# Retention and a routed MLP on one core: the order of loads, weights and gathers around the first batches

## The chip, the core and the metric

The kernel runs on one core of a Trainium2 chip. Its engines are TensorE (PE in the profile, with its weight loads as PEld), VectorE (DVE), ScalarE (ACT), GpSimd (POOL) and SyncE (SP), and a core has 16 DMA engines. The metric is the device time of one execution in microseconds, lower is better; times are medians of several executions.

## The reference

Two blocks follow each other. The first is retention in its parallel form: 8 batches, 8 heads, 576 positions, head size 64. The second is a mixture of depths: of each batch's 576 tokens the 128 with the highest gate score go through an MLP (512 to 1024 to 512), and all others pass unchanged. All is float32.

```python
scores = scale * np.matmul(q, k.transpose(0, 1, 3, 2))
Dmat = np.where(rel >= 0, gamma[:, None, None] ** rel[None, :, :], 0.0)
attn_out = np.matmul(scores * Dmat[None], v)
x = attn_out.transpose(0, 2, 1, 3).reshape(B, S, H * D)
...
scores = np.einsum('bsd,d->bs', x, w_gate)
for b in range(B):
    top_idx = np.argpartition(-scores[b], capacity)[:capacity]
    xe = x[b, top_idx]
    ye = np.maximum(xe @ w1, 0.0) @ w2
    g = 1.0 / (1.0 + np.exp(-scores[b, top_idx]))
    out[b, top_idx] = xe + g[:, None] * ye
```

## The kernel before

**Steps.** The 576 positions of a batch are 9 chunks of 64, and a step handles two chunks, so the 8 batches are 36 steps; a step can hold the end of one batch and the start of the next. Retention is done chunk by chunk: within a chunk by a masked product of queries and keys (`sc_ps`, masked on DVE into `am`, multiplied with the values into `y_ps`), across chunks by a running state (`u_ps`, copied by ACT to `st`). The decay is put into the values by GpSimd (`scaled`, line 187, writes `vs`) and into the result afterwards (`values`, line 266, writes `xs`). A step needs one load of 1 MB (`raw`: queries, keys, values, keys again) and stores 256 KB of result to HBM (`stored`, line 286).

**What one step emits.** The main loop (line 487) emits, in this order: the scaling for step s+1; the matmuls of step s together with those of `y_ps` of step s-1; the stores of step s-2; then `values` for step s-1, the planned work of the lists `first`, `soon` and `mid`; then some parts of an MLP; then the lists `late` and `then`. The engines PE, DVE, ACT and SP run their instructions in the order in which they are emitted (line 136, `ENGINES` in line 25). GpSimd isn't in that set: a scheduler sets the order of its instructions.

**Routing and MLP of a batch.** `values` adds up each token's gate score on DVE (line 283). When a batch is complete, its scores are put into one row of every partition (`flatten`, `spread`), `compare` counts for each token how many are ahead of it, `one_hot` turns the counts into a selection matrix (`hot`), and `fetch` (line 367) multiplies it with the token numbers (`idx_ps`, `idx`) and starts an indirect DMA on GpSimd, which gathers the 128 chosen rows (`xr`) from the result in HBM. `mlp` (line 426) first transposes the rows (`turn`, `xg_ps`), then queues eight parts: four `up` (two blocks of `h_ps` each) and four `down` (`ye_ps`). `some(n)` runs the next n of them, and n spreads the parts over the steps that remain until the next batch's MLP is ready (line 508). At the end `o` is scattered back into HBM by a second indirect DMA on GpSimd (line 419).

**Plan.** Lines 439 to 484 fix for each batch the step of each of these. With s the step in which a batch is complete, batch 0 gets its `fetch` inside the matmuls of step s+3 = 8 and its MLP inside those of step s+5 = 10. For the others `when` gives steps after s; its last entry is the MLP.

**Loads and weights.** Five loads are issued at the start. After that `pe` (line 113) counts instructions of TensorE. Each time the count passes another 256 (`BLOCK`, with an offset), it may start one due piece of the weights (eight of 512 KB, from step 5 on, one per step) and one load, if the loads are less than 4 steps ahead of the current one. Such a transfer waits until the matmul at that place is done (`start`, line 107), and all of them go through SyncE's queue in order. `quiet` skips one such place after a fetch of batch 1 or later.

## Time and profile before

| what | value |
|---|---|
| median of 3 runs | 258.6 us (258.28 to 261.3) |
| span of the profiled execution | 258.1 us |
| PE busy | 225.4 us (87%) |
| PEld busy | 174.8 us (68%) |
| DVE busy | 151.2 us (59%) |
| ACT busy, POOL busy | 59.3 us, 59.6 us (23% each) |
| HBM read, written | 44.67 MB, 11.53 MB: 218 GB/s over the span |

The page cuts the span into 40 slices of 6.45 us. A digit is the busy share in tenths (9 is 90% or more), PEclk the clock that TensorE was granted, in tenths of full speed, and the last line what DMA moved.

```profile
PE   8565785689889989896999999999999999999991
PEclk9889979759999999999999999999999999999999
DMA  6999899998666776881778985888876303111101
GB/s 210 403 324 341 260 339 372 379 390 273 212 226 226 234 266 229 289 283 64 235 241 288 301 288 169 263 259 296 285 251 227 99 17 80 44 41 41 43 0 41
```

Up to the eighth slice DMA is nearly full and PE half idle. From the ninth slice on PE is full except around the nineteenth, where DMA moved little as well.

### The profile page before, as it was taken

Reading aid. Unit: us, or ns where it says so; the run is one execution under the profiler, and the core shown is the slowest. Engines: PE = TensorE matmul, PEld = TensorE weight load, DVE = VectorE, ACT = ScalarE, POOL = GpSimd, SP = SyncE. Lnnn points to the kernel's source line nnn. Section 1 sums busy time; section 2 is a strip of 40 time slices with the busy share of each in tenths; the row PEclk is TensorE's granted clock in tenths of the full one; section 3 lists DMA queues with packets and bytes.
Section 4 is the critical chain, followed back from the end, with each engine's and each line's share of the span. In section 5 each row is a group of like instructions: output and inputs, shape, how many; then the busy total and the mean of one; then the engine's idle time right before and its main releaser. Section 6 shows DMA issues by size and latency. Waiting matters only on the chain.

```text
span 258.1 us, 11373 instructions
## 1 busy us (share of the span) xinstructions
PE 225.4 (87%) x5102; PEld 174.8 (68%) x5102; DVE 151.2 (59%) x436; ACT 59.3 (23%) x178; POOL 59.6 (23%) x59
## 2 busy tenths in 40 slices
PE   8565785689889989896999999999999999999991
PEld 3564574579755887555985799568966895784940
DVE  0156788542885536973983699579944861950201
ACT  1125443112510223112221321122211220211200
POOL 3333113312141112133131150413312210101101
PEclk9889979759999999999999999999999999999999
DMA  6999899998666776881778985888876303111101
GB/s 210 403 324 341 260 339 372 379 390 273 212 226 226 234 266 229 289 283 64 235 241 288 301 288 169 263 259 296 285 251 227 99 17 80 44 41 41 43 0 41
DMA packets 20945, 56.95 MB, mean 221 GB/s; under 512 B 2336, under 2 KB 13984, under 8 KB 16416
## 3 DMA queue, kind: packets, MB, share of 16 engines
q1 hardware_dynamic: 19616, 52.02, 59.9%
q0 software_dynamic: 1280, 4.20, 4.6%
q8 instruction: 40, 0.66, 1.0%
q14 instruction: 9, 0.07, 0.1%
HBM read 44.67 MB, written 11.53 MB: 218 GB/s over the span
## 4 chain that ended last, share of the span: by engine, by line
PE 51%; issue 24%; DMA 20%; POOL 2%; POOLq 1%; SPq 0%; DVE 0%
PE h_ps L134 14%; DMA raw<-in_qkvk 10%; PE ye_ps L134 9%; PE u_ps L134 8%; DMA xr<-out,idx 8%; PE sc_ps L134 8%; PE y_ps L134 7%; PE row_ps L134 3%; DMA w_sb<-in_w 2%; PE xg_ps L394 1%; POOL out L419 1%; POOL xr L375 1%; POOL vs L189 1%; POOLq L584 0%; SPq L108 0%
## 5 line engine op out<-in xcount | busy, mean ns | idle before, releaser
L189 POOL TENSOR_TENSOR vs<-raw,table 128x512 f32<-128x512 f32 x36 | 40.1, 1113 | 140.2 <-DMA raw<-in_qkvk 105.1
L134 PE MATMUL h_ps<-xg,w_sb 128*128 128x128 f32 x512 | 61.9, 280 | 0.1
L134 PEld LDWEIGHTS h_ps<-xg,w_sb 128*128 128x128 f32 x512 | 59.6, 195 | 2.2 <-issue 1.2
L134 PE MATMUL ye_ps<-w_sb,hT 128*128 128x512 f32 x128 | 60.1, 605 | 0.0
L134 PE MATMUL u_ps<-vs,raw 64*64 64x64 f32 x1024 | 45.9, 229 | 7.3 <-POOL vs L189 3.1
L262 DVE TENSOR_TENSOR am<-sc_ps,table 128x512 f32<-128x512 f32 x36 | 24.8, 688 | 45.5 <-PE sc_ps L134 26.5
L134 PE MATMUL y_ps<-vs,am 64*64 64x64 f32 x1152 | 46.1, 229 | 5.3 <-issue 4.8
L134 PEld LDWEIGHTS u_ps<-vs,raw 64*64 64x64 f32 x1024 | 37.8, 140 | 18.6 <-issue 12.8
L134 PE MATMUL sc_ps<-raw 64*64 64x64 f32 x1152 | 45.3, 228 | 4.4 <-issue 4.1
L134 PEld LDWEIGHTS sc_ps<-raw 64*64 64x64 f32 x1152 | 40.4, 143 | 9.2 <-issue 7.9
L209 ACT COPY st<-u_ps 128x256 f32<-128x256 f32 x64 | 24.0, 375 | 90.0 <-PE u_ps L134 59.9
L134 PEld LDWEIGHTS y_ps<-vs,am 64*64 64x64 f32 x1152 | 39.5, 141 | 5.4 <-issue 4.8
L134 PE MATMUL y_ps<-st,raw 64*64 64x64 f32 x1024 | 39.9, 226 | 0.9 <-issue 0.8
L283 DVE SCALAR_TENSOR_TENSOR scr<-xs,wg_half 128x256 f32<-128x256 f32 x72 | 34.8, 483 | 6.6 <-ACT xs L272 4.1
L350 DVE SCALAR_TENSOR_TENSOR scr<-row,tok,ahead 128x576 f32<-128x576 f32 (+2 forms) x49 | 36.2, 739 | 2.8 <-ACT row L326 0.8
L134 PEld LDWEIGHTS ye_ps<-w_sb,hT 128*128 128x128 f32 x128 | 22.7, 190 | 21.1 <-issue 20.1
L134 PEld LDWEIGHTS y_ps<-st,raw 64*64 64x64 f32 x1024 | 35.8, 141 | 1.3 <-issue 1.2
L275 DVE TENSOR_TENSOR xs<-y_ps,table 128x512 f32<-128x512 f32 x31 | 21.1, 682 | 7.4 <-PE y_ps L134 7.4
L406 ACT ACTIVATE hT<-h_ps 128x256 f32<-128x256 f32 x32 | 12.3, 384 | 49.1 <-PE h_ps L134 49.1
L343 DVE SCALAR_TENSOR_TENSOR scr<-row,table 128x128 f32<-128x128 f32 (+1 forms) x40 | 12.7, 317 | 14.9 <-ACT row L326 14.2
L418 DVE SCALAR_TENSOR_TENSOR o<-ye_ps,gate,xr 128x512 f32<-128x512 f32 x8 | 6.0, 750 | 24.4 <-issue 12.7
L419 POOL DMA_INDIRECT out<-o,idx x8 | 9.0, 1130 | 35.2 <-DVE o L418 32.5
(32 smaller groups left out, 106.2 us busy)
## 6 DMA issues: line engine op xcount, KB each, us to landing
raw<-in_qkvk SPq DMA_DIRECT2D x35, 1024.0 KB, 5.4
out<-xs SPq DMA_DIRECT2D x64, 128.0 KB, 5.5
w_sb<-in_w SPq DMA_DIRECT2D x8, 512.0 KB, 6.5
raw<-in_qkvk SPq DMA_DIRECT2D x2, 512.0 KB
out<-xs SPq DMA_DIRECT2D x16, 64.0 KB, 6.3
wg<-in_w_gate SPq DMA_DIRECT2D x1, 256.0 KB
table<-in_consts SPq DMA_DIRECT2D x1, 130.5 KB
wg_half<-in_w_gate SPq DMA_DIRECT2D x2, 64.0 KB, 7.3
```

Of the source, the lines that this page charges most:

```text
L134: return pe(nc.tensor.matmul(out, lhsT, rhs, **more), 4 if lhsT.dtype == F32 else 2)
L189: nc.gpsimd.tensor_tensor(out=four(vs[s]), in0=four(raw[s][:, 2, :]), in1=factor(s, 0), op=OP.mult)
L209: nc.scalar.copy(out=st[b, c], in_=u_ps[b][:, :W])
L262: nc.vector.tensor_tensor(out=am[s], in0=sc_ps[s].rearrange("p (h d) -> p h d", h=H), in1=causal.unsqueeze(1).to_broadcast([P, H, C]), op= ...
L275: nc.vector.tensor_tensor(out=four(xs[s]), in0=four(y_ps[s]), in1=factor(s, 1), op=OP.mult)
L283: nc.vector.scalar_tensor_tensor(scr[:, :W], part, 1.0, wg_half, op0=OP.mult, op1=OP.mult, accum_out=sc[b][:, c : c + 1])
L343: nc.vector.scalar_tensor_tensor(scr[:, :n], row[b][:, P * j : P * j + n], 1.0, eye[:, :n], op0=OP.mult, op1=OP.mult, accum_out=tok[b][:, ...
L350: nc.vector.scalar_tensor_tensor(scr[:, : i1 - i0], row[b][:, i0:i1], tok[b][:, j : j + 1], ahead[:, at + i0 : at + i1], op0=OP.subtract, ...
L375: nc.gpsimd.indirect_dma_start(out=xr[b], out_offset=None, in_=outs[b], in_offset=bass.IndirectOffsetOnAxis(ap=idx[b][:, :1], axis=0))
L406: nc.scalar.activation(out=hT[b][:, f : f + n, :], in_=t[:, :n, :], func=AF.Relu)
L418: nc.vector.scalar_tensor_tensor(o, ye[b], gate[b], xr[b], op0=OP.mult, op1=OP.add)
L419: nc.gpsimd.indirect_dma_start(out=outs[b], out_offset=bass.IndirectOffsetOnAxis(ap=idx[b][:, :1], axis=0), in_=o, in_offset=None)
```

## The change

The change reorders transfers and work; it computes the same.

- Four loads instead of five are issued at the start, the row of the gate (`wg`) in step 4 instead of 1. From step 5 on, while weights are still to come, loads keep 3 steps ahead instead of 4. The weights' pieces are due from step 6 on.
- GpSimd joins the engines whose order is as emitted, and `scaled(s + 1)` is emitted after the matmuls of step s, so that a `fetch` inside them stands ahead of it. After the fetch of batch 0 transfers that `pe` would start are held (`hold`), and released behind the next scaling.
- `fetch` of the batches from 1 on is planned at the end of its step (`late`) instead of in `mid`, except where the batch is cut in two parts. The MLPs of batches 1 and 2 are planned one step later.
- The gate scores of steps 5 and 6 (`BEHIND`) are added up later, so that DVE can do batch 0's selection first. The table `ahead` of GpSimd and the copy of `place` are made a little later.

```diff
-ENGINES = {ET.PE, ET.DVE, ET.Activation, ET.SP}
+ENGINES = {ET.PE, ET.DVE, ET.Activation, ET.SP, ET.Pool}
...
     def start(out, in_, behind):
+        if behind is not None and now["hold"]:
+            held.append((out, in_))
+            return
...
-            if now["load"] < NS and lead < 4:
+            if now["load"] < NS and lead < (4 if now["step"] < FEW or not weights else 3):
...
     load()
-    load()
     nc.sync.dma_start(out=table[:, n_first:], in_=consts[:, n_first:])
...
-        weights.append((5 + f // 2, w1_sb[:, :, e], w1[:, e].rearrange("(a p) f -> p a f", p=P)))
+        weights.append((6 + f // 2, w1_sb[:, :, e], w1[:, e].rearrange("(a p) f -> p a f", p=P)))
...
-        weights.append((9 + f // 2, w2_sb[:, f : f + 2, :],
+        weights.append((10 + f // 2, w2_sb[:, f : f + 2, :],
...
+    BEHIND = [(NC - 1) // 2 + 1, (NC - 1) // 2 + 2]
...
+        if s not in BEHIND:
+            scored(s)
+
+    def scored(s):
...
-        now["quiet"] = int(b > 0)
+        now["quiet"], now["hold"] = int(b > 0), int(b == 0)
...
+            for r in BEHIND:
+                plan(soon, s + 2, scored, r)
...
-            when = 1, (1, 1, 1, 2, 2), 2, 3, 4
+            when = 1, (1, 1, 1, 2, 2), 2, 3, 5
         else:
-            when = 1, (1, 1, 2, 2, 3), 3, 4, 5 + int(b > 2)
+            when = 1, (1, 1, 2, 2, 3), 3, 4, 6
...
-        plan(mid, s + when[3], fetch, b)
+        plan(mid if last else late, s + when[3], fetch, b)
...
-        if s == 1:
+        if s == 4:
             nc.sync.dma_start(out=wg, in_=spread_out(0, DM, P))
...
+        matmuls(s)
         if s + 1 < NS:
-            scaled(s + 1)
-        matmuls(s)
+            ins = scaled(s + 1)
+        now["hold"] = 0
+        while held:
+            start(*held.popleft(), ins)
+        if s == 1:
+            order_of_places()
```

`FEW` is 5. `order_of_places` holds the two GpSimd instructions that make `ahead`; the copy of `place` moves from step 1 to step 2.

## The prediction

> **What bounds the kernel now.** I read the waits of TensorE first: they add up to little (about 27 us) and name the reasons. Columns: engine and line, what it waited for, us in total, times, longest.

> ```profile
> PE y_ps L134 <- issue: 5.6, 6, 1.8
> PE idx_ps L134 <- DVE hot L360: 4.2, 3, 1.9
> PE sc_ps L134 <- issue: 4.1, 4, 1.6
> PE xg_ps L394 <- DMA xr<-out,idx: 3.9, 3, 2.9
> PE u_ps L134 <- POOL vs L189: 3.1, 3, 1.3
> ```

> "issue" is a wait that the profile cannot name. It falls in the middle of a step, and each time a 16 KB transfer of the instruction queue ended some 1.4 us before PE went on. So I read it as PE waiting for its next block of instructions.

> Then stages. I cut the span where the first "sc" matmul of a step falls: 43.95 is step 8, 54.46 step 10, 84.0 step 14, 120.7 step 20. Columns: length, busy us of PE, PEld, DVE, ACT, POOL, then granted clock, DMA share, GB/s.

> ```profile
> 11.00:43.95 32.95, 21.49 (x890) 18.77 (x890) 22.21 (x66) 13.54 (x55) 7.50 (x8) 0.90 0.96 330
> 43.95:54.46 10.51, 7.29 (x246) 6.20 (x245) 6.38 (x15) 1.18 (x4) 3.86 (x4) 0.73 1.02 386
> 54.46:84.00 29.54, 27.65 (x574) 21.43 (x576) 17.69 (x48) 7.33 (x18) 6.35 (x6) 0.92 0.73 252
> 84.00:120.70 36.70, 31.26 (x835) 24.26 (x829) 22.24 (x64) 8.23 (x23) 9.85 (x9) 1.00 0.72 239
> 120.70:209.00 88.30, 87.16 (x2158) 69.89 (x2153) 67.01 (x194) 20.40 (x58) 22.20 (x20) 1.00 0.72 235
> 209.00:258.00 49.00, 43.48 (x378) 30.44 (x370) 14.97 (x48) 6.58 (x20) 5.31 (x5) 0.99 0.13 39
> ```

> Until step 10 DMA is full (0.96 to 1.02) and PE idles 11.46 + 3.22 = 14.7 us: there is only attention to do, and its data arrive at DMA's pace. From step 10 on PE is the bound. What it still loses is 1.9 us in steps 10 to 13 and 5.4 us in steps 14 to 19; then 1.1 us in 88, and the end (5.5 us), which the change doesn't touch.

> The 1.9 and 5.4 us are named by the single gaps of PE: 1.11 us at 73.8 and 1.24 us at 108.3 before "idx" (it waits for "hot" of batches 1 and 2), 2.87 us at 115.8 before "xg" (it waits for the gather of batch 2). GpSimd shows why that gather was late:

> ```profile
> 111.75 1.57 POOL L189 TENSOR_TENSOR vs<-raw,table 128x512 f32<-128x512 f32 x1 [5.37 <-DMA raw<-in_qkvk]
> 113.47 0.99 POOL L375 DMA_INDIRECT xr<-out,idx  x1 [0.15 <-DMA raw<-in_qkvk]
> ```

> Its index was there at about 110.1, but a scaling that waited for a load stood ahead of it. Batch 0 has the same picture, and its gather takes 8 us beside full DMA (the chain that ended last):

> ```profile
> 39.77 5.64 DMA w_sb<-in_w
> 45.41 7.96 DMA xr<-out,idx
> 53.37 0.04 issue
> 53.41 1.12 PE xg_ps L394 x4
> ```

> [...] its half-speed stretches are 11.30 to 14.72, 31.78 to 35.20 and 48.85 to 59.09, all multiples of 3.41. The last costs real work: from 53.41, when batch 0's MLP starts, to 59.09 PE is never idle and does half. [...] The trace has the blocks (40 packets, 0.66 MB, on a queue of their own) [...]. [...]

> **The change, part by part.**

> *Four loads first, the gate row later.* 1 MB and 0.25 MB leave the first queue. Loads 0 and 1 lie ahead of them and are unmoved, so step 1 still starts at 11.0. Load 4 now goes in step 1 (at about 12.5); at the 385 to 400 GB/s of that stage it lands by about 17.5, before 19.3. Step 4 needs it at 22. Cost nothing; some of the instruction blocks behind loads start earlier. Of the stalls at 19.7, 23.4 and 28.6 (1.07, 1.84, 1.26) I take 0.1 + 0.6 + 0.3 = 1.0 us off (bounds 0 and 2.0, the part above the 1.07 that recurs at 15.8, 19.7 and 38.0).

> *Lead of three, weights from step 6.* In step 5 the lead is 3, so no load goes; load 8 goes in step 6 behind the first weight, load 9 in step 7, each one step later than now. DMA is nearly empty when the block of step 6 is fetched, so the 1.07 us at 38.0 goes. Step 6 then comes 1.0 and step 7's middle 2.0 us earlier. But the slack of loads is spent. Now load 8 is issued at 30.72 and scaled at 39.34, 4.6 us ahead of step 8's sc. After: weight at 34.4 - 1.2 = 33.2, load at 33.8. A load alone takes 5.0 to 5.4 us to land, 0.5 MB ahead of it 1.3 us at 386 GB/s, part of it overlapped: landed 39.4, scaled (1.04) by 40.5. Step 8's sc waits for "hot" anyway, 43.95 - 2.0 = 42. Load 9: weight at about 38, both behind load 8 and a store in the queue (1.76 MB at 386 GB/s = 4.6 us after load 8's data at 38.9), landed about 44.3, scaled 45.4. Step 9's sc at 46.0, now 46.73.

> *Gather first, loads held.* In the changed order GpSimd has the gather of batch 0 between scalings 8 and 9. Index at about 42.3, gather issued at 42.5 instead of 45.41; with 5.0 to 5.5 us it lands near 48, not 53.37. The price: the third weight and load 10 wait until scaling 9 is done, 45.4, instead of going at 40.40. Behind them on SyncE stand the stores and load 11; TensorE waits for load 10 through scaling 10. Issued at 45.9, landed at 45.9 + 5.4 = 51.3 [...], scaled at 52.4, step 10 at 52.5, xg at about 53.0. So the 0.84 us wait for the gather and the "hot" wait of 1.89 us are replaced by waits for loads 9 and 10; sum 0.4 us earlier (bounds: 2.1 us later if the 1.0 + 1.07 don't come, 2 us earlier).

> *Clock.* [...] 3.41 us at half speed, 1.7 us of work. Bounds +1.7 and -1.7, taken as 0.8 us gained[...].

> *Later batches later.* The fetch moves behind the step's MLP part (1.9 us per part). "hot" of batch 1 was 1.11 us late and of batch 2 1.24 us: both fit behind it. The MLPs of batches 1 and 2 go one step later (14 and 20 instead of 13 and 19), the gather stands ahead of the next scaling: issued near 110.5, landed near 115.6, needed after 118. All of 1.11 + 1.24 + 2.87 = 5.2 us goes (bounds 2.5 and 5.5). Work of PE is unchanged, and PE is full afterwards, so this shows in the end time.

> *What that costs.* Batch 0's MLP is spread over steps 10 to 14 (3, 2, 1, 1, 1 parts; now 3, 2, 2, 1). Steps 12 to 14 have 2.1 us of attention, 1.9 of MLP and 0.5 of copies, some 4.7 us, beside 1.76 MB per step, 4.6 us. DMA is full again, instruction blocks are late again: 1.0 us lost (bounds 0 and 3, one stall per step).

> *At nothing.* The postponed "scored" of steps 5 and 6 (four of 0.48 us): DVE idled 0.94 us ahead of "am" of step 7, so they weren't on the path. The order table and "place" move among idle GpSimd and DVE.

> Sum: 258.6 - 0.4 - 0.8 - 5.2 + 1.0 = 253.2.

> **Rivals.**
> - *Both halves gain (249.7).* Instruction stalls before step 7 go by 2.0 more and the clock returns one window earlier, with no new stalls: 258.6 - 2.0 - 1.7 - 5.2 = 249.7. For: "issue" is the largest group of waits. Against: loads 9 and 10 then bind.
> - *Gain eaten by loads (258.2).* Step 10 at 55.5, not 53.4 (+2.1), half speed one window longer (+1.7), stalls in steps 12 to 14 (+1.0), waits saved (-5.2): 258.2, no change. For: a slack of 4.6 and 2.9 us for loads 8 and 9 against one step of 4.5 us taken away.
> - *Slower (264.2).* Each of loads 8, 9 and 10 costs 1.5 us (+4.5), the clock 1.7, stalls +2.0, only half of the 5.2 saved: 258.6 + 4.5 + 1.7 + 2.0 - 2.6 = 264.2. Against: PE has 3 us of fetch stalls there that a shorter queue gives back.

> **How the numbers follow.** Forecast 0.48, both gain 0.20, eaten 0.24, slower 0.08. Two per cent is 253.4, close to the forecast: about half of its 0.48 lies on each side. Faster 0.47, same 0.45, slower 0.08. The range takes the ends of the two neighbours: 248.8 to 258.4.

> **What would show it.** Right: "hot" and the gather gone from PE's waits; the gather of batch 0 under 6 us and issued before 43.5; step 10 between 52 and 54.5; PE over 99% busy in steps 14 to 20; PE waits on vs up, to 2 to 5 us, in steps 8 to 10. Wrong: step 10 after 55.5, or half speed after 59.1, or new waits for weights in steps 11 to 14.

## The result: slower, 1.046 times the time before

The changed kernel takes 272.1 us (median of 4 executions, 269.71 to 273.22). The kernel before, measured beside it, takes 259.95 us (258.28 to 261.51). The ratio is 1.0456 with a 95% interval from 1.0343 to 1.0569. That is far outside the predicted range of 248.8 to 258.4 us. Executions of one kernel here can lie 1 to 5% apart; ratios rest on the undisturbed ones, so a ratio can differ a little from that of the medians, and some runs have none.

**The page.** These are the same four rows as before, now in 40 slices of 6.78 us. Look at the clock row: a 5, half speed throughout, stands in slices 6 and 8 to 10, where before only the ninth had one. The DMA row has holes (5 and 4) in slices 6 and 8, where it had a 9 in both.

```profile
PE   8658484938989989998799999998999999999991
PEclk9967957555999999999999999999999999999998
DMA  6978959495678984787786666677768512111101
GB/s 221 404 284 280 282 172 311 147 370 192 243 259 305 388 305 141 271 263 242 276 262 226 237 221 193 216 226 251 241 213 258 186 42 77 41 39 39 41 0 40
```

**The waits of TensorE** (engine and line, what it waited for, us in total, times, longest):

```profile
PE u_ps L138 <- POOL vs L197: 16.7, 11, 5.6
PE y_ps L138 <- issue: 6.8, 10, 2.9
PE sc_ps L138 <- issue: 3.6, 4, 2.3
PE u_ps L138 <- issue: 2.0, 4, 0.6
PE xg_ps L406 <- DMA xr<-out,idx: 0.2, 1, 0.2
```

The wait for "hot" (4.2 us) is gone and the one for the gather has shrunk from 3.9 to 0.2 us: what the change aims at, it does. But TensorE now waits 16.7 us for the scaled values `vs`, where it waited 3.1 us. A scaling waits for its load, so this is a wait for DMA with GpSimd's name on it.

**The stages**, cut again at the first "sc" of steps 8, 10, 14, 20 and 35 (length, busy us of PE, PEld, DVE, ACT, POOL, then clock, DMA share, GB/s):

```profile
11.00:48.98 37.98, 24.76 (x889) 22.00 (x889) 21.71 (x66) 13.53 (x55) 10.43 (x9) 0.75 0.82 277
48.98:64.04 15.06, 9.03 (x246) 8.01 (x245) 5.69 (x15) 1.18 (x4) 3.20 (x3) 0.50 0.76 274
64.04:90.63 26.59, 25.13 (x567) 20.15 (x569) 16.67 (x47) 6.96 (x17) 5.31 (x5) 0.94 0.73 249
90.63:124.60 33.97, 30.85 (x830) 24.38 (x825) 24.41 (x65) 8.07 (x22) 8.94 (x8) 1.00 0.80 272
124.60:221.80 97.20, 91.71 (x2174) 72.76 (x2169) 69.82 (x195) 20.96 (x59) 23.16 (x22) 1.00 0.67 220
221.80:271.00 49.20, 43.37 (x370) 30.33 (x362) 15.02 (x49) 6.47 (x19) 5.34 (x5) 0.98 0.13 38
```

Against the lengths of before this is +5.0 us to step 8, +4.6 in steps 8 and 9, -3.0 in steps 10 to 13, -2.7 in steps 14 to 19, +8.9 in steps 20 to 34 and +0.2 at the end: +13.0, the difference of the spans (271.1 and 258.1). Two things stand out. The first two stages lost 9.6 us, and DMA, which had been their bound at a share of 0.96 and 1.02, is at 0.82 and 0.76. And the gain of steps 10 to 19 came (-5.7), but steps 20 to 34 took it back.

**Where DMA was idle.** Windows of the changed kernel, then the same windows of the kernel before:

```profile
35.00:37.50 2.50, 1.86 (x53) 1.59 (x46) 1.93 (x6) 0.07 (x1) 0.91 (x1) 0.50 0.07 21
37.50:49.00 11.50, 6.99 (x202) 6.06 (x202) 7.49 (x24) 4.62 (x20) 1.70 (x1) 0.65 0.93 305
49.00:54.00 5.00, 4.62 (x133) 4.25 (x136) 2.58 (x7) 0.62 (x3) 2.17 (x2) 0.50 0.32 102
```

```profile
35.00:37.50 2.50, 1.94 (x80) 1.61 (x83) 2.42 (x9) 1.47 (x7) 0.00 (x0) 0.96 0.93 296
37.50:49.00 11.50, 5.99 (x290) 5.16 (x280) 8.26 (x25) 3.96 (x18) 3.80 (x4) 0.99 1.03 371
49.00:54.00 5.00, 3.48 (x89) 3.13 (x89) 3.01 (x7) 0.37 (x1) 0.72 (x2) 0.50 1.04 391
```

From 35 to 37.5 us DMA moves 21 GB/s instead of 296: everything issued has landed, and the next load may not go until TensorE is further. From 49 to 54 us it has little to do again (102 instead of 391 GB/s), this time with load 10 held back until 53.00. Nothing in these two stages makes the time up.

**Why TensorE waits at step 10.** The chain of the changed kernel that ended last, between the two holes and step 10 (start, us, what; SPq is the issue of a DMA on SyncE's queue):

```profile
42.18 0.39 SPq L112
42.66 8.67 DMA raw<-in_qkvk
51.40 0.10 issue
51.50 1.05 POOL vs L197
52.56 0.39 SPq L112
53.00 7.68 DMA raw<-in_qkvk
60.75 0.10 issue
60.84 1.04 POOL vs L197
61.93 0.37 PE u_ps L138 x2
63.06 1.04 PE xg_ps L406 x4
```

Load 9 takes 8.67 us to land behind a weight, then comes its scaling, and only that scaling lets the held weight (52.56) and load 10 (53.00) go; load 10 takes 7.68 us more. Two loads that used to overlap stand one behind the other. In the kernel before, load 10 went at 40.40 and was scaled at 48.42; now 53.00 and 60.84. GpSimd's own timeline shows the same scalings:

```profile
45.85 1.70 POOL L197 TENSOR_TENSOR vs<-raw,table 128x512 f32<-128x512 f32 x1 [9.93 <-DMA w_sb<-in_w]
49.54 1.13 POOL L387 DMA_INDIRECT xr<-out,idx  x1 [1.99 <-ACT st L217]
51.50 1.04 POOL L197 TENSOR_TENSOR vs<-raw,table 128x512 f32<-128x512 f32 x1 [0.83 <-DMA raw<-in_qkvk]
60.84 1.03 POOL L197 TENSOR_TENSOR vs<-raw,table 128x512 f32<-128x512 f32 x1 [8.31 <-DMA raw<-in_qkvk]
```

The 9.93 us before the scaling of step 8 hold the first hole and then the landing of load 8, which goes at 37.29 (the profile names the weight issued just ahead of it); the 8.31 us before that of step 10 are the landing of load 10. The gather does stand ahead of a scaling, as intended, but at 49.54 instead of 45.41, since its index was later still. TensorE's gaps are 3.95 us at 43.7 (step 8) and 5.65 us at 56.3 (step 10).

### The profile page after: what moved, and what is told of

It is laid out like the page before. It is cut to its first block, busy times and chain, and to the rows that moved or that the text cites. A ratio compares the mean times of both kernels' runs of the same rounds, so it can differ in the third digit from the quotient of the medians.

```text
span 271.1 us, 11368 instructions
## 1 busy us (share of the span) xinstructions
PE 232.6 (86%) x5102; PEld 181.6 (67%) x5102; DVE 154.0 (57%) x436; ACT 59.2 (22%) x178; POOL 58.9 (22%) x59
## 4 chain that ended last, share of the span: by engine, by line
PE 52%; issue 24%; DMA 16%; POOL 4%; SPq 2%; POOLq 1%; ACT 1%; DVE 0%
DMA raw<-in_qkvk 16%; PE h_ps L138 14%; PE ye_ps L138 11%; PE u_ps L138 9%; PE sc_ps L138 8%; PE y_ps L138 7%; POOL vs L197 3%; PE row_ps L138 2%; SPq L112 1%; POOL xr L387 1%; PE xg_ps L406 1%; SPq L151 1%; POOL out L431 0%; POOLq L603 0%; PE idx_ps L138 0%
## 5 line engine op out<-in xcount | busy, mean ns | idle before, releaser
L138 PE MATMUL u_ps<-vs,raw 64*64 64x64 f32 x1024 | 47.7, 237 | 19.9 <-POOL vs L197 16.7
L138 PEld LDWEIGHTS h_ps<-xg,w_sb 128*128 128x128 f32 x512 | 59.1, 193 | 2.5 <-issue 1.5
L138 PEld LDWEIGHTS u_ps<-vs,raw 64*64 64x64 f32 x1024 | 39.9, 149 | 29.9 <-POOL vs L197 19.6
L138 PE MATMUL y_ps<-vs,am 64*64 64x64 f32 x1152 | 51.6, 239 | 7.1 <-issue 6.8
L138 PE MATMUL sc_ps<-raw 64*64 64x64 f32 x1152 | 51.0, 238 | 4.0 <-issue 3.6
L138 PEld LDWEIGHTS y_ps<-vs,am 64*64 64x64 f32 x1152 | 43.6, 149 | 9.4 <-issue 9.0
L138 PEld LDWEIGHTS sc_ps<-raw 64*64 64x64 f32 x1152 | 44.5, 151 | 6.4 <-issue 4.7
L138 PE MATMUL y_ps<-st,raw 64*64 64x64 f32 x1024 | 42.7, 237 | 0.1
L138 PEld LDWEIGHTS y_ps<-st,raw 64*64 64x64 f32 x1024 | 38.7, 152 | 1.1 <-issue 1.1
L295 DVE SCALAR_TENSOR_TENSOR scr<-xs,wg_half 128x256 f32<-128x256 f32 x72 | 34.0, 472 | 6.8 <-ACT xs L280 4.3
L138 PEld LDWEIGHTS ye_ps<-w_sb,hT 128*128 128x128 f32 x128 | 22.7, 190 | 21.3 <-issue 20.1
L355 DVE SCALAR_TENSOR_TENSOR scr<-row,table 128x128 f32<-128x128 f32 (+1 forms) x40 | 17.3, 431 | 11.0 <-ACT row L338 10.3
```

Source lines behind the costliest of these rows:

```text
L138: return pe(nc.tensor.matmul(out, lhsT, rhs, **more), 4 if lhsT.dtype == F32 else 2)
L295: nc.vector.scalar_tensor_tensor(scr[:, :W], part, 1.0, wg_half, op0=OP.mult, op1=OP.mult, accum_out=sc[b][:, c : c + 1])
L355: nc.vector.scalar_tensor_tensor(scr[:, :n], row[b][:, P * j : P * j + n], 1.0, eye[:, :n], op0=OP.mult, op1=OP.mult, accum_out=tok[b][:, ...
```

## The experiments

The theory after the result: the new loads (four at the start, a lead of three, weights one step later) starve DMA, and the hold makes it worse. The rivals: the hold alone; GpSimd's fixed order; the later plan of the batches. The runs were made in four groups, each on one chip and with its own runs of the kernel before. "Step 10" below is the first "sc" of step 10, in the profiled execution. The kernel before was profiled in the first measurement only, so where its step 10 stands beside a run of a group, it comes from another chip. Repeats, and runs whose executions scatter too far for an interval, are partly left to the text.

| kernel | group | median us (before) | ratio, 95% | step 10 | DMA share 30 to 50 us |
|---|---|---|---|---|---|
| before | first measurement | 258.6 | | 54.5 | 0.98 |
| changed | first measurement | 272.1 (259.95) | 1.046 [1.034, 1.057] | 64.0 | 0.77 |
| changed, no hold | 1 | 261.94 (261.5) | 1.003 [0.994, 1.011] | 59.2 | 0.79 |
| changed, old loads | 1 | 259.23 (261.5) | 0.993 [0.986, 1.000] | 53.9 | 0.97 |
| changed, no hold, old GpSimd | 1 | 262.24 (261.5) | 0.999 [0.988, 1.009] | 59.0 | 0.84 |
| before + later plan | 1 | 258.63 (261.5) | 0.990 [0.982, 0.998] | 56.1 | 0.96 |
| before + new loads | 2 | 267.84 (261.3) | 1.027 [1.017, 1.036] | 60.0 | 0.77 |
| before + four loads, weights from 6 | 3 | 266.31 (261.6) | 1.029 [1.014, 1.043] | 58.9 | 0.89 |
| before + lead of three | 3 | 265.25 (261.6) | none | 62.1 | 0.81 |
| changed | 3 | 272.49 (261.6) | 1.033 [1.017, 1.050] | 61.6 | 0.80 |
| changed, no hold | 4 | 264.16 (260.9) | 1.015 [0.999, 1.030] | 61.0 | 0.73 |
| changed, old loads | 4 | 257.44 (260.9) | 0.980 [0.965, 0.996] | 54.5 | 0.93 |
| before + GpSimd order | 4 | 258.98 (260.9) | 0.994 [0.991, 0.998] | 54.6 | 0.97 |

### First group: which part of the change costs

*The changed kernel without the hold.*

```diff
-        now["quiet"], now["hold"] = int(b > 0), int(b == 0)
+        now["quiet"] = int(b > 0)
```

> The changed kernel without the hold: what is due after the fetch of batch 0 goes at once. Theory (DMA is left idle ahead of step 10, by the shorter lead and by the hold): load 10 goes some 3 us earlier than its 53.0, the first sc matmul of step 10 falls at about 61 instead of 64.0, and the time is 268 to 270 against 272.1. Rival (GpSimd's order as emitted is what delays the scalings and so TensorE): nothing changes, 271 to 273. The gather of batch 0 may get slower again, towards 8 us; TensorE doesn't wait for it.

Measured 261.94 us against 261.5 for the kernel before, 1.0028 [0.9943, 1.0114]. Load 10 is issued at 47.4 instead of 53.0 and step 10 starts at 59.2. The theory's number missed: the time came almost level with the kernel before. But step 10 was still 4.8 us later than before, so the hold could not be all, and the second half of this run was better than in the first measurement (steps 20 to 34 in 90.5 us, not 97.2). The changed kernel itself had not run on this chip, so what follows from this run alone is little; the third group repeats it beside the changed kernel.

*The changed kernel with the old loads, hold kept.*

```diff
+    load()
-            if now["load"] < NS and lead < (4 if now["step"] < FEW or not weights else 3):
+            if now["load"] < NS and lead < 4:
-        weights.append((6 + f // 2, ...
+        weights.append((5 + f // 2, ...
-        weights.append((10 + f // 2, ...
+        weights.append((9 + f // 2, ...
```

> The changed kernel with the loads and weights of before: five loads at the start, a lead of four throughout, weights due from step 5. The hold, GpSimd's order and the later batches stay. Theory (idle DMA): step 8's first sc is back at about 44 instead of 49.0, DMA stays over 0.9 busy up to there, half speed shrinks from 20 us to about 10, and the time falls by 8 to 10 us to 262 to 264; what remains above the time before is the hold. Rival (GpSimd's order): step 8 and 10 stay late, 270 to 272.

Measured 259.23 us, 0.993 [0.9859, 1.0002]. Step 10 starts at 53.9, as in the kernel before, with the hold in place. DMA's share from 30 to 50 us is back at 0.97 (340 GB/s). So with the old loads the hold does no harm that shows at step 10. The run without the hold, on the same chip, took 2.7 us more in the medians, but the two intervals overlap: what the new loads cost in time isn't settled by this group.

*The changed kernel without the hold, and GpSimd as before* (out of `ENGINES`, `scaled(s + 1)` ahead of `matmuls(s)`).

```diff
-ENGINES = {ET.PE, ET.DVE, ET.Activation, ET.SP, ET.Pool}
+ENGINES = {ET.PE, ET.DVE, ET.Activation, ET.SP}
-        matmuls(s)
         if s + 1 < NS:
             ins = scaled(s + 1)
+        matmuls(s)
```

> The changed kernel without the hold, and with GpSimd outside the engines whose order is as emitted and the scaling of step s+1 emitted before the matmuls of step s, as before. To be read against the run that lacks the hold alone. Theory: GpSimd's order costs only the waits of 1 us each in steps 14, 15, 20, 21 and later (4.4 us in all after step 10), so 264 to 268. Rival (GpSimd's order is the main cause): 258 to 261, with step 10 back near 54.

Measured 262.24 us, 0.9989 [0.9884, 1.0094], step 10 at 59.0: the same as without the hold alone (261.94, 59.2). GpSimd's order is not the cause.

*The kernel before with only the later plan.*

```diff
-            when = 1, (1, 1, 1, 2, 2), 2, 3, 4
+            when = 1, (1, 1, 1, 2, 2), 2, 3, 5
-            when = 1, (1, 1, 2, 2, 3), 3, 4, 5 + int(b > 2)
+            when = 1, (1, 1, 2, 2, 3), 3, 4, 6
-        plan(mid, s + when[3], fetch, b)
+        plan(mid if last else late, s + when[3], fetch, b)
```

> The kernel before with the later plan alone: the fetch at the end of its step, the MLPs of batches 1 and 2 one step later. The prediction put this part at 5.2 us saved: the waits for hot of batches 1 and 2 (1.1 and 1.2 us) and for the gather of batch 2 (2.9 us) vanish, so 253.5 to 255.5 where the kernel before takes 258.6 to 260. Rival (the later plan gives back what it saves, because steps 12 to 14 have too little work to hide loads and blocks of instructions): 257 to 260.

Measured 258.63 us, 0.9902 [0.9821, 0.9984]: a gain, of 2.9 us in the medians (2.6 by the ratio), where the prediction had 5.2. The waits for "hot" and for the gathers of batches 1 and 2 are gone. Steps 10 to 19 take 58.6 us instead of 66.2, but steps 20 to 34 take 93.1 instead of 88.3. About 2.4 us of that is work that now falls there: four more "ye" matmuls (1.8 us: the groups by line for these steps have 22.7 us for 48 on the old plan and 24.5 us for 52 on the new one) and four transposes "xg" (0.6 us). Another 2.05 us is one wait of TensorE at 151.9 us, named "issue" in the profile; it ended 1.27 us after a 16 KB block of instructions had arrived.

### Second group: the new loads alone

*The kernel before with the new loads alone* (the reverse of the second edit above, on the kernel before).

```diff
-    load()
-            if now["load"] < NS and lead < 4:
+            if now["load"] < NS and lead < (4 if now["step"] < 5 or not weights else 3):
-        weights.append((5 + f // 2, ...
+        weights.append((6 + f // 2, ...
-        weights.append((9 + f // 2, ...
+        weights.append((10 + f // 2, ...
```

> The kernel before with four loads at the start, the lead of three while weights come, and weights from step 6; nothing else. Theory (DMA is left idle in the stage that it bounds): step 8's first sc at 45.5 to 49, step 10's at 57 to 60 instead of 54.5, half speed longer, time 1.01 to 1.025 of before. Rival (the shorter queue gives the instruction blocks back as much as it takes): 0.995 to 1.005.

Measured 267.84 us, 1.0267 [1.0173, 1.0361]. This part alone makes the kernel slower; it is the clearest comparison of the study. The waits of TensorE in this run are led by the same one as in the changed kernel, and one is of its own:

```profile
PE u_ps L134 <- POOL vs L188: 11.2, 6, 6.3
PE idx_ps L134 <- DVE hot L359: 3.6, 3, 1.3
PE ye_ps L134 <- DMA w_sb<-in_w: 3.2, 1, 3.2
```

The 6.3 us is at step 10, which starts at 60.0, with no hold and no fixed order of GpSimd in the kernel. The hole in DMA is there too, 26 GB/s from 33 to 35 us (same columns as the stages):

```profile
33.00:35.00 2.00, 1.70 (x69) 1.38 (x60) 1.97 (x6) 0.37 (x1) 1.06 (x1) 0.63 0.08 26
35.00:37.50 2.50, 2.07 (x34) 1.45 (x34) 2.39 (x11) 0.60 (x3) 0.00 (x0) 0.50 0.89 290
```

The wait of 3.2 us for the last weights belongs to this mix: the MLP is still on the early plan while its weights come a step later. The changed kernel, whose plan is later, doesn't have it. So this run overstates the cost of the new loads in the changed kernel by up to 3.2 of its 6.5 us.

*The changed kernel again,* on this chip:

> The changed kernel unaltered, on the chip of the other runs of this set. The run without the hold came out at 1.003 of the kernel before, where the changed kernel had 1.046, but in profile it was quicker also in steps 1 to 8, ahead of any hold, and in steps 20 to 35. If the hold alone costs it: again 1.04 to 1.05, with step 10 at 62 to 65. If the loads cost it and the difference lay in the conditions of the run: 1.01 to 1.03.

Its executions took 267.43 to 278.35 us, median 274.08, beside 261.32 for the kernel before; they lie too far apart for an interval. Step 8 starts at 48.9 and step 10 at 64.1, as in the first measurement.

*The changed kernel with the hold released earlier*: the held transfers go behind ACT's copy of the index instead of behind the scaling.

```diff
-            start(*held.popleft(), ins)
+            start(*held.popleft(), now["idx"])
```

> The changed kernel with the held transfers released behind ScalarE's copy of the index instead of behind GpSimd's next scaling: they stand at the same place of SyncE's queue, but no longer wait for load 9. Theory (the hold costs since it makes load 10 wait until load 9 has landed and is scaled, one after the other): as without the hold, 1.00 to 1.01. Rival (the hold costs by the place in the queue, or there is another cause): 1.03 to 1.05.

Its median is 270.05 us (265.41 to 272.03, no interval). Load 10 goes at 49.6 instead of 53.8 and step 10 starts at 61.3 instead of 64.1. In this pair of traces the hold costs some 3 us at step 10. What is left is 6.8 us later than in the kernel before on its chip, and 3.9 us later than in the next run, the only one with the old loads on this chip.

*The changed kernel with neither hold nor new loads* (both edits of the first group):

> The changed kernel without the hold and with the loads and weights of before; GpSimd's order, the postponed gate scores and the later batches stay. Against the run that had the old loads and the hold (0.993): if the hold costs several us by itself, 0.96 to 0.98. If it costs only where the lead is three, because then nothing else is queued in DMA: 0.985 to 0.995.

Its executions took 258.38, 263.06, 263.94 and 271.2 us, too far apart to say anything about the time. Step 10 started at 57.4, ahead of every run with the new loads, but 2.9 us behind the kernel before (54.5). Beside the new loads alone on this chip (60.0), they cost 2.7 us at step 10, not the 5.5 us that the first measurement's kernel before suggests.

### Third group: the lead or the weights, and the hold side by side

*The kernel before with four loads at the start and weights from step 6, lead of four kept.*

```diff
-    load()
-        weights.append((5 + f // 2, ...
+        weights.append((6 + f // 2, ...
-        weights.append((9 + f // 2, ...
+        weights.append((10 + f // 2, ...
```

> The kernel before with four loads at the start and the weights due from step 6, but a lead of four throughout: load 8 goes in step 5 as before. Theory (late loads leave DMA idle, and the lead alone makes them late): 0.995 to 1.005, step 8's first sc at 43 to 45. Rival (weights a step later delay batch 0's MLP, or the fifth load was needed): 1.01 to 1.03.

Measured 266.31 us, 1.0287 [1.0142, 1.0432]. Here the loads come in time: load 10 goes at 42.5. The time is lost elsewhere. The gather of batch 0 is issued at 48.7 and TensorE waits 4.17 us for it at 53.6; it waits 2.47 us for the last weights at 85.0. (The 2.94 us for the gather of batch 2 at 121.6 are no loss: the kernel before waits 2.87 us there.) I had taken these two edits to cost nothing. Together they do, at least on the early plan of the MLPs. Which of the two costs, and whether the longer wait for the first gather comes from them, no run shows. And with the lead of three added (second group) the ratio was no higher: 1.027.

*The kernel before with the lead of three alone.*

```diff
-            if now["load"] < NS and lead < 4:
+            if now["load"] < NS and lead < (4 if now["step"] < 5 or not weights else 3):
```

> The kernel before with the lead of three while weights come, nothing else: five loads at the start, weights from step 5. Load 8 goes in step 6 and not 5, every load until step 12 one step later. Theory: this part makes most of the 1.027 that the three edits on loads and weights cost together: 1.015 to 1.03, waits of TensorE for scalings of 5 us and more in steps 8 to 10. Rival: 0.995 to 1.005.

Executions took 260.22 to 266.11 us, median 265.25; there is no interval. Those of the kernel before beside it took 256.78 to 265.54, so in time the cost of the lead alone isn't shown. The trace is clear about the place: load 8 goes at 35.8 (30.7 before), TensorE waits 6.08 us at 40.7 (step 8) and 6.1 us at 53.9 (step 10) for scalings, and step 10 starts at 62.1. That is the picture of the changed kernel up to step 10, from one number.

*The changed kernel and the changed kernel without the hold,* side by side:

> The changed kernel unaltered, side by side with the one that lacks only the hold. The run without the hold had 1.003 on another chip than the changed kernel, and the two differed also where their code is the same, so the price of the hold is open. Expected: 1.03 to 1.05.

> The changed kernel without the hold. By what the two differ between step 8 and step 10 in the profiles (15.1 us with the hold, 12.4 to 13.4 with the transfers released earlier) the hold costs 2 to 3 us: 1.02 to 1.04 on this chip, if the rest of the earlier difference was the chip; 1.00 to 1.01 if the hold costs 10 us.

272.49 us (1.0334 [1.0168, 1.0499]) with the hold, 270.41 us (265.62 to 275.43, no interval) without. The difference of 2.1 us in the medians is smaller than the scatter of either. Step 10 starts at 61.6 and 61.2. On this chip no cost of the hold shows; it isn't the main cause, and the near-level time of the first group was not due to its absence alone.

### Fourth group: the parts that gain

*The kernel before with only GpSimd's order changed* (the reverse of the third edit).

> The kernel before with GpSimd among the engines whose order is as emitted and the scaling of step s+1 after the matmuls of step s; loads, weights and plan as before, no hold. Batch 0's gather then stands between scalings 8 and 9 as in the changed kernel. Theory: nothing waits for GpSimd while loads come early, and the gather is issued about 1.5 us earlier: 0.99 to 1.00. Rival (the order itself makes TensorE wait for scalings in steps 14 to 35): 1.01 to 1.02.

Measured 258.98 us over 20 executions, 0.9944 [0.9909, 0.9979]: a gain of about half a per cent.

*The later plan alone,* again:

> The kernel before with the later plan alone, once more on a chip of this set. It had 0.990. If the later plan is a gain by itself: 0.98 to 0.995 again. If it is one only where instruction blocks arrive fast, as they did in all four runs of that set (steps 23 to 34 without stalls of 0.9 us): 0.995 to 1.01, with such stalls in steps 28, 30, 32, 34.

Measured 259.22 us, 0.9885 [0.9727, 1.0043], in line with the first group's 0.990.

*The changed kernel with the old loads,* again:

> The changed kernel with the loads and weights of before, hold kept, once more on a chip of this set (0.993 before). If the loads and weights are the main cause of the loss on any chip: 0.99 to 1.01, at least 2 per cent under the run with the new loads beside it.

*The changed kernel without the hold,* again:

> The changed kernel without the hold, a third time (1.003 on the first chip, 270.4 against 261.6 us in the medians on another). Beside the old loads on the same chip it shows what loads and weights cost: 1.02 to 1.04 if that is 5 to 8 us, as the first matmul of step 10 says (59 to 61 against 54 to 57).

With the old loads 257.44 us, 0.9804 [0.9649, 0.996]; without the hold 264.16 us, 1.0146 [0.9992, 1.0301]. Beside each other on one chip the two intervals don't overlap, and the medians are 6.7 us apart. What TensorE waited for from 30 to 62 us, in the kernel without the hold and then in the one with the old loads:

```profile
PE u_ps L138 <- POOL vs L197: 7.5, 3, 3.5
PE y_ps L138 <- issue: 2.1, 1, 2.1
PE idx_ps L138 <- DVE hot L372: 1.2, 1, 1.2
PE sc_ps L138 <- issue: 1.2, 1, 1.2
PE u_ps L138 <- issue: 1.1, 2, 0.6
```

```profile
PE y_ps L138 <- issue: 4.9, 2, 3.5
PE sc_ps L138 <- issue: 2.8, 3, 1.9
PE u_ps L138 <- issue: 2.5, 4, 0.8
PE idx_ps L138 <- DVE hot L373: 1.5, 1, 1.5
PE u_ps L138 <- POOL vs L198: 0.8, 1, 0.8
```

With the old loads the scalings are in time (0.8 us of waiting instead of 7.5). What remains is "issue", 10.2 us in its three rows instead of 4.4. Part of it falls in step 10 itself, and so the first "sc" of step 10 overstates what the new loads cost. In these two traces step 10 is 6.5 us apart (61.0 and 54.5), step 14 2.1 us (88.7 and 86.6), the whole span 2.2 us (262.0 and 259.8; the latter is the slowest of its four executions). In the first group it is 5.4 us at step 10, 1.5 at step 14 and 2.2 in the span.

The change as a whole less its new loads comes out at 0.980 here (0.987 by the medians of all executions) and 0.993 in the first group, so a gain of some 1 to 2% over the kernel before. The later plan alone, at 0.990 and 0.989, isn't clearly worse.

## Why the prediction was wrong

The forecast was 253.2 us. It fails in the step **"Lead of three, weights from step 6"**, and what the later steps build on it falls with it. That step had loads 8 and 9 in time and step 8 at 42; step 8 came at 48.98, and step 10, forecast at 52.5, at 64.04. A second term, **"What that costs"**, missed by nearly as much.

- **The time from issue to landing.** I took 5.0 to 5.4 us for a load alone and 1.3 us for the 0.5 MB ahead of it, partly overlapped. That put the landing of load 8 5.6 us after its issue. It was 8.56 us to the start of its scaling (37.29 to 45.85), with DMA empty when it went. Load 9 took 8.8 us, load 10 7.8 us. The kernel before had the number: its load 8 was issued at 30.72 and scaled at 39.34, as the prediction itself says, which is 8.62 us; its loads 9 and 10 took 8.86 and 8.02 us. The 5.4 us is a median over the eight loads whose landing the profile has. Five of these, at 5.0 to 5.5 us, were issued after 121 us; load 8 is the only one from the stage in question, at 8.47. In the traces of both kernels and of the new loads alone none of loads 8 to 10 took less than 6.8 us from issue to scaling.
- **The time of issue.** I had load 8 at 33.8; it went at 37.3. The stalls that I took off before step 6 didn't go: in place of 1.08, 1.07, 1.84 and 1.26 us there were 2.35 us at 14.7, 0.83 us at 24.6 and 2.91 us at 28.7, and step 6 started 1.5 us later than before, not 1.0 us earlier. TensorE was at half speed from 33.3 to 43.5, which delays the place in its instructions where the load is due. "Cost nothing" was right for load 4 (scaled at 19.1, before at 19.3), not for the stalls.
- **No margin.** The prediction itself worked out that loads 8 and 9 have 4.6 and 2.9 us of slack and that a step of 4.5 us is taken away. It then put the result "in time" into the forecast and "late" into a rival with 0.24. A full DMA was read as the bound and yet the part of the change that empties it was costed at nothing; that is the error of reasoning behind the sizes.
- **"Gather first, loads held".** I had load 10 issued at 45.9 and scaled by 52.4; it was 53.0 and 61.9, since scaling 9, on which it hangs, ended 7.1 us later than I had it (52.5 instead of 45.4). The exchange that the prediction described, a wait for the gather replaced by waits for loads 9 and 10, is what happened. The sum to step 10, -0.4 us, was +9.6 us. Of this the hold accounts for about 3 us by the second group's run and next to nothing by the third's.
- **"Clock".** Forecast 0.8 us gained, my estimate for one stretch of 3.41 us less at half speed. Half speed lasted from 33.3 to 43.5 and from 47.0 to 67.4; over the first 70 us it is 37.5 us instead of 17. The first of the two stretches follows the stall of 2.91 us, the second the wait for the scaling of step 8 (the windows are in the last section). Half speed lengthens what the waits leave (an `h` matmul took 427 ns on average from 64.02 to 67.44, and 285 ns from 67.44 to 70.85), and no run separates its share.
- **"Later batches later", right in mechanism, too large in size.** "hot" and the gathers left TensorE's waits as forecast (but for 0.2 us), and the stages of steps 10 to 19 became 5.7 us shorter. But 2.9 us of this is less work in these steps (56.0 us busy instead of 58.9), much of it moved into steps 20 to 34; idle time fell by 2.8 us, not 5.2. PE was busy 91% of steps 14 to 19, not over 99%, since waits for scalings came in (1.06 us at 123.0, for one). Alone, the later plan brought 2.6 and 3.0 us by its two ratios, the second with an interval that reaches 1.
- **"What that costs".** Forecast 1.0 us lost, in steps 12 to 14, with 3 at most. Measured +8.9 us in steps 20 to 34, for which the prediction has no term: it took what is saved before step 20 to hold to the end. That is a miss of 7.9 us, of which 2.4 is work moved there, beside one of 10.0 us up to step 10.
- **GpSimd's order**, not on the path by the forecast apart from the gather, gains 0.6% alone. Weights from step 6 with four loads at the start were taken as harmless, and these two edits together cost 2.9%.
- **The rivals.** "Slower (264.2)" named the right cause, each of loads 8 to 10 late and the clock with it, but with 1.5 us per load and 0.08 of chance. Of its three terms, the loads were mis-sized most: 4.5 us against the 9.6 us by which step 10 is late (the clock included).

**What stays open.** Steps 20 to 34 took 97.2 us, where the kernel before took 88.3. About 2.4 us is work that the later plan moves there, 2.1 us are two waits for scalings, and the rest, some 4.4 us, goes with steps 23, 28, 30, 32 and 34, each 0.8 to 0.9 us longer than in the fourth group's kernel without the hold, with an "issue" gap of about 0.4 us in each. On the chips of groups 2 and 3 the changed kernel and its variants took 96.0 to 100.6 us in these steps; on those of groups 1 and 4 they took 90.5 to 91.1, while kernels with the new loads but the old plan took 89.1 to 89.9 in groups 2 and 3. So part of the loss, 5 to 10 us, appears on some chips only. It isn't the new loads or the hold, since the second group's kernel with neither took 96.0; it comes with the later plan, GpSimd's order or the smaller moves, and why is not settled. Late instruction blocks don't explain the gaps: in steps 23, 28, 30 and 32 the last block had ended 4.6 to 6.0 us before TensorE went on, while after the long stalls of the first 60 us it was some 1.4 us (only step 34 has 1.25). The conclusion on the loads rests on what happens up to step 10 in the traces and on comparisons within one chip. It bears on the loss up to step 10 of the first measurement, not on the 8.9 us behind it.

## What to carry to other kernels

Where DMA's share is near 1, count what a change does to the number of transfers in flight before counting anything else: here a lower lead showed first as a hole in DMA's share, then as a wait for whatever engine stands between the load and TensorE. Price a load by issue to use as the trace of the kernel before has it in that stage (here 8.0 to 8.9 us), not by a median over the run (5.4), and compare that with the slack before moving it by a step. Time that a stage saves is a gain only if the stages behind it don't grow: here 5.7 us came off steps 10 to 19 and 8.9 us came on in steps 20 to 34. And test a bundle of edits part by part: here two parts gained 0.6% and about 1% alone, a third, the hold, cost 0 to 3 us at step 10, and the new loads cost 2.7% alone.

## What the runs showed of the hardware

```profile
40.13:43.54 3.41, 3.41 (x128) 3.34 (x127) 0.71 (x2) 1.64 (x8) 0.00 (x0) 0.50 0.92 302
43.54:46.96 3.42, 0.12 (x6) 0.00 (x0) 3.28 (x11) 2.02 (x9) 1.11 (x1) 1.00 1.00 326
50.37:53.78 3.41, 3.03 (x84) 2.65 (x81) 1.93 (x5) 0.00 (x0) 1.34 (x2) 0.50 0.30 97
64.02:67.44 3.42, 3.42 (x75) 3.29 (x75) 1.35 (x3) 0.86 (x2) 1.04 (x1) 0.50 0.24 46
67.44:70.85 3.41, 3.41 (x38) 3.22 (x38) 1.50 (x6) 0.76 (x2) 0.00 (x0) 1.00 0.97 356
```

  After the window with 3.41 us of work (from 40.13) the clock was full, after the one with 0.12 it was half. From 46.96 on, five windows with 2.77, 3.03, 2.50, 0.00 and 2.08 us of work left the clock at half, and here only a full one, from 64.02, was followed by full speed, at 67.44. The busy time of one window doesn't settle the clock of the next: in the kernel before, half speed followed 1.57 us (from 28.37) and 1.86 us (from 45.44) but not 1.65 us (from 21.54), and in the changed kernel 2.92 us at half speed (from 19.65) was followed by full speed, where 3.03 us was not.
- Some stalls of TensorE that the profile names "issue" ended soon after a 16 KB block of the instruction queue had arrived: in the changed kernel those of 2.35 us at 14.7 and 2.91 us at 28.7 ended 1.37 and 1.28 us after one. That TensorE waited for the block is my reading. In the fourth group's pair the two "issue" rows before "y" and "sc" have 7.7 us from 30 to 62 us with a DMA share of 0.93 from 30 to 50 us, and 3.3 us with 0.73. That a full DMA is the reason is not shown by a run.
